# Group normalization on one core: transfers in runs of three, a part of the sums from TensorE to VectorE, and GpSimd's share of the scaling to VectorE

## The chip, the cores and the metric

The kernel runs on one core of a Trainium2 chip, alone. The metric is the device time of one execution in microseconds (us), the median of several executions. The time before the change was 633.9 us (633.54 to 634.19 in three runs).

## The reference

x has the shape (128, 1024, 32, 16) in bf16: 128 samples, 1024 channels in 32 groups. Each group of each sample (32 channels of 512 elements) is normalized with its own mean and variance, then each channel is scaled and shifted.

```python
G = 32
xr = x.reshape(B, G, C // G, H, W)
mu = xr.mean(axis=(2, 3, 4), keepdims=True)
var = ((xr - mu) ** 2).mean(axis=(2, 3, 4), keepdims=True)
xn = (xr - mu) / jnp.sqrt(var + 1e-5)
return xn.reshape(B, C, H, W) * g[None, :, None, None] + b[None, :, None, None]
```

The input and the output are 134 MB each, so the kernel must move 268.4 MB through the core's DMA engines. There is little arithmetic per byte.

## The kernel before

A tile has 128 partitions (4 samples x 32 groups) and 16384 columns (32 channels x 512), which is 4 MB. There are 32 tiles and six buffers. Per tile, TensorE sums the columns by multiplying 32 chunks of 512 columns with the identity into 512 columns of PSUM, VectorE reduces these to the mean, ScalarE squares the tile in two halves and sums the squares, and then 32 channels are scaled in place: 16 on VectorE, 13 on GpSimd, 3 on ScalarE. All loads and stores are issued from one queue (SP). The order of transfers is: six loads, then two stores, two loads, two stores, and so on ("runs of two").

```python
XBUFS = 6; UPFRONT = 6; RUN = 2; LAST_SHARE = 3; POOL_SHARE = 13
...
def matmuls(st, name, lo, hi):          # sums of chunks lo..hi-1 in PSUM
    ps = pspool.tile([P, MMN], F32, name=name)
    for k in range(lo, hi):
        nc.tensor.matmul(out=ps[:], lhsT=eye[:], rhs=st["xt"][:, k*MMN:(k+1)*MMN], ...)
...
def A(i):                               # scale the channels of tile i
    if not in_parts(i):                 # all but the last two tiles
        for n in range(POOL_SHARE):
            scale_on("pool", i, KC - LAST_SHARE - POOL_SHARE + n)
        for k in range(KC - LAST_SHARE - POOL_SHARE):
            scale_on("dve", i, k)
        ...
def finish(i):
    for k in range(KC - LAST_SHARE, KC):
        scale_on("act", i, k)           # one instruction per channel
    S(i, 0, NQ)                         # store tile i
    if i % RUN == RUN - 1:              # after each run of stores: a run of loads
        first = i + 1 + UPFRONT - RUN
        for j in range(first, min(first + RUN, NT)):
            L(j)
...
for i in range(NT):
    Q(i)                                # squares of tile i, finish(i - 1) in between
    if i + 1 < NT:
        M(i + 1); R0(i + 1)             # sums and mean of the next tile
    V(i)                                # variance, scale and shift of tile i
    A(i)
```

## Time and profile before

| | before |
|---|---|
| time, span in the profile | 633.9 us, 632.5 us |
| DMA | mean 425 GB/s over the span, 432 in the middle |
| ACT, DVE, POOL, PE busy | 85%, 60%, 55%, 41% |

In the views of the profile PE is TensorE and PEld its weight loads, DVE is VectorE, ACT is ScalarE, POOL is GpSimd, SP issues the transfers, and L368 is line 368 of the kernel. Here are three lines of the profile page of the kernel before: the busy time of each engine, and for 40 equal slices of the span the busy tenths of the DMA engines and what they moved.

```profile
PE 260.9 (41%) x1025; PEld 106.4 (17%) x1025; DVE 379.0 (60%) x645; ACT 537.9 (85%) x268; POOL 345.3 (55%) x523
...
DMA  9999999999999999999999999999999999999996
GB/s 371 437 428 406 436 433 431 433 429 433 429 424 433 429 437 431 432 434 433 434 432 424 432 433 431 429 432 432 431 431 431 436 429 432 431 425 435 431 423 260
```

DMA is at 9 (90% or more) in every slice but the last. The windows view says the same for the long middle part; its columns are each engine's busy time with its count of instructions, then TensorE's granted clock, the DMA share and GB/s.

```profile
core 0: us, PE busy (x) PEld busy (x) DVE busy (x) ACT busy (x) POOL busy (x), PEclk, DMA share, GB/s
113.00:543.00 430.00, 178.81 (x704) 72.86 (x704) 269.73 (x431) 379.11 (x185) 260.03 (x388) 0.71 1.00 432
```

So in this window the DMA share is 1.00, and every other engine has some time to spare (ACT, the busiest, is at 85% over the span). The next fence is from the DMA queues of the page (packets, bytes, share of the engines' time). Queue q1 carries the tiles; q8 and q14 carry instructions, in packets of 16 KB (q8) and 8 KB (q14), and the page counts their time with that of the same 16 DMA engines: 0.1% and 0.0%.

```profile
q1 hardware_dynamic: 10944, 268.44, 99.0%
q8 instruction: 8, 0.13, 0.1%
q14 instruction: 15, 0.12, 0.0%
```

The next fence has groups of instructions of the page, with busy time in all and the mean of one in ns.

```profile
L244 ACT ACTIVATE ja<-xt,negmean 128x8192 fp8e5<-128x8192 bf16 x60 | 426.6, 7109 | 55.2 <-DVE jd L189 55.1
...
L368 DVE TENSOR_SCALAR xt<-xt,scl,bia 128x512 bf16<-128x512 bf16 x536 | 351.4, 730 | 39.8 <-POOL bia L353 39.8
L368 POOL TENSOR_SCALAR xt<-xt,scl,bia 128x512 bf16<-128x512 bf16 x390 | 307.5, 801 | 3.4 <-POOL bia L353 0.3
...
L189 DVE TENSOR_SCALAR_CACHE_REDUCE jd<-pa 128x512 bf16<-128x512 f32 x32 | 21.9, 684 | 113.9 <-PE pa L166 113.9
```

One scaling instruction lasts 730 ns on VectorE and 801 ns on GpSimd here. On VectorE they overlap, so its pace is 0.66 us a channel (351.4 us over 536). The timeline of VectorE near the end shows the same 16 instructions once beside GpSimd (first line) and once alone (second line; the last two tiles use no GpSimd).

```profile
start us, us, engine line op out<-in xcount [idle before <-releaser]
574.64 11.11 DVE L368 TENSOR_SCALAR xt<-xt,scl,bia 128x512 bf16<-128x512 bf16 x16 [1.28 <-POOL bia L353]
...
591.62 5.26 DVE L368 TENSOR_SCALAR xt<-xt,scl,bia 128x512 bf16<-128x512 bf16 x16 [1.28 <-POOL bia L353]
```

They take 11.11 us beside GpSimd and 5.26 us alone: 0.69 against 0.33 us a channel. Why VectorE is slower beside GpSimd is not shown by the traces.

**Reading the landings.** In the trace each of the 76 loads and stores has 16 increments of its semaphore, and the page counts 16 DMA engines. I read each increment as the landing of one engine's share. That is my reading: the trace names no engine beside an increment. It fits the rate, as the first increments of loads that follow each other are 9.71 us apart, and 4.19 MB in 9.71 us is the 432 GB/s of the windows view. The times of the increments were read from the stored trace with a short script, as no view of the profile lists them. Sorted, they show how far the slowest DMA engine lags behind the fastest, though not which engine it is. For the last store of the kernel before, in us after the first of the 16 (which landed at 624.18):

```
0.00 0.05 0.21 0.82 1.56 1.62 1.71 1.71 1.84 2.97 3.13 3.22 4.13 5.26 7.03 7.36
```

In the first loads the lag is 0.5 us. The rest is built up in jolts (tiles for which the slowest engine takes 0.2 to 1.2 us longer than for the others), and the kernel ends with the slowest engine, at 631.54 us. The fastest engine takes 9.66 to 9.72 us for nearly every tile, with no gap.

### The profile page before, as it was taken

How to read it: one execution, taken by the hardware profiler on the slowest of the kernel's cores; microseconds unless marked ns; L12 is line 12 of the kernel's file. 1: busy time of each engine (PE TensorE's matmuls, PEld its weight loads, DVE VectorE, ACT ScalarE, POOL GpSimd, SP SyncE). 2: the span in 40 equal slices, each digit the busy share in tenths (PEclk: the TensorE clock that was granted, in tenths of full speed). 3: DMA queues.
4: the chain of work that ended last, by engine and by line, in shares of the span. 5: the costliest groups of instructions: out<-in, count | busy, mean ns of one | idle time of the engine just before them, and what ended most of it. 6: DMA issues, size and time to landing. Idle time of an engine off the chain costs nothing.

```text
span 632.5 us, 3907 instructions
## 1 busy us (share of the span) xinstructions
PE 260.9 (41%) x1025; PEld 106.4 (17%) x1025; DVE 379.0 (60%) x645; ACT 537.9 (85%) x268; POOL 345.3 (55%) x523
## 2 busy tenths in 40 slices
PE   5577609064180632806327063270723607146000
PEld 2223203021030210302113021030301203012000
DVE  1077766666676477563665636666466663657660
ACT  4599999999999699696996969969798796987960
POOL 0077776666666377563665636666365663657100
PEclk9789759668595675957759577595875958758555
DMA  9999999999999999999999999999999999999996
GB/s 371 437 428 406 436 433 431 433 429 433 429 424 433 429 437 431 432 434 433 434 432 424 432 433 431 429 432 432 431 431 431 436 429 432 431 425 435 431 423 260
DMA packets 11063, 268.70 MB, mean 425 GB/s; under 512 B 1312, under 2 KB 1312, under 8 KB 1312
## 3 DMA queue, kind: packets, MB, share of 16 engines
q1 hardware_dynamic: 10944, 268.44, 99.0%
q8 instruction: 8, 0.13, 0.1%
q14 instruction: 15, 0.12, 0.0%
q10 hardware_dynamic: 96, 0.00, 0.0%
HBM read 134.22 MB, written 134.22 MB: 424 GB/s over the span
## 4 chain that ended last, share of the span: by engine, by line
DMA 62%; ACT 15%; PE 9%; issue 5%; DVE 3%; POOL 2%; SPq 0%; DVEq 0%; ACTq 0%; POOLq 0%
DMA out_dram<-xt 40%; DMA xt<-in_x_dram 21%; ACT ja L244 13%; PE pa L166 9%; DVE xt L368 3%; ACT xt L363 2%; POOL xt L368 1%; DMA gb_b<-in_g_dram 0%; ACT rstd L308 0%; POOL scl L337 0%; POOL shift L343 0%; POOL bia L353 0%; SPq L101 0%; DVE rstd L312 0%; DVE jd L189 0%
## 5 line engine op out<-in xcount | busy, mean ns | idle before, releaser
L244 ACT ACTIVATE ja<-xt,negmean 128x8192 fp8e5<-128x8192 bf16 x60 | 426.6, 7109 | 55.2 <-DVE jd L189 55.1
L166 PE MATMUL pa<-xt,eye 128*128 128x512 bf16 x976 | 250.1, 421 | 317.9 <-DMA xt<-in_x_dram 317.9
L368 DVE TENSOR_SCALAR xt<-xt,scl,bia 128x512 bf16<-128x512 bf16 x536 | 351.4, 730 | 39.8 <-POOL bia L353 39.8
L368 POOL TENSOR_SCALAR xt<-xt,scl,bia 128x512 bf16<-128x512 bf16 x390 | 307.5, 801 | 3.4 <-POOL bia L353 0.3
L166 PEld LDWEIGHTS <-eye 128*128 128x128 bf16 x1024 | 106.3, 106 | 472.2 <-DMA xt<-in_x_dram 318.8
L337 POOL TENSOR_SCALAR scl<-gb,rstd 128x32 f32<-128x32 f32 x31 | 11.1, 358 | 220.1 <-DVE rstd L312 220.1
L189 DVE TENSOR_SCALAR_CACHE_REDUCE jd<-pa 128x512 bf16<-128x512 f32 x32 | 21.9, 684 | 113.9 <-PE pa L166 113.9
L363 ACT ACTIVATE xt<-xt,bia,scl 128x512 bf16<-128x512 bf16 x98 | 72.0, 799 | 0.8 <-DVE bia L324 0.8
L312 DVE RECIPROCAL rstd<-rstd 128x1 f32<-128x1 f32 x32 | 5.2, 163 | 72.7 <-ACT rstd L308 72.7
L244 ACT ACTIVATE ja<-xt,q 128x4096 fp8e5<-128x4096 bf16 x8 | 29.7, 3706 | 6.6 <-DVE jd L189 6.4
L343 POOL TENSOR_SCALAR shift<-scl,negmean 128x32 f32<-128x32 f32 x31 | 11.1, 358 | 3.1
L216 POOL TENSOR_SCALAR off<-negmean,q 128x1 f32<-128x1 f32 x2 | 0.9, 430 | 20.4 <-DVE jd L189 20.4
L166 PE MATMUL pb<-xt,eye 128*128 128x512 bf16 x48 | 11.0, 379 | 0.6 <-DMA xt<-in_x_dram 0.6
L244 ACT ACTIVATION_READ_ACCUMULATOR ja<-xt,negmean 128x1 f32 x60 | 11.2, 187 | 0.0
L308 ACT ACTIVATE rstd<-s,v 128x1 f32<-128x1 f32 x30 | 8.8, 294 | 2.8
L353 POOL TENSOR_TENSOR bia<-shift,gb 128x32 f32<-128x32 f32 x31 | 7.8, 251 | 2.6
L273 POOL TENSOR_SCALAR v<-s 128x1 f32<-128x1 f32 x30 | 5.7, 191 | 2.5
L308 ACT ACTIVATE rstd<-var,eps_t 128x1 f32<-128x1 f32 x2 | 0.6, 294 | 7.5 <-DVE jv L292 7.5
L156 DVE COPY gb<-gb_p 128x64 f32<-128x64 f32 x1 | 0.2, 225 | 5.5 <-PE gb_p L148 5.5
L116 ACT ACT_TABLE_LOAD x1 | 1.3, 1283 | 1.7 <-PEq L445 1.7
L189 DVE DVE_READ_ACCUMULATOR jd<-pa 128x1 f32 x32 | 2.6, 80 | 0.0
L292 DVE TENSOR_SCALAR_CACHE_REDUCE jv<-sq,seed 128x4 f32<-128x4 f32 x2 | 0.4, 214 | 2.7 <-ACT ja L244 2.7
(18 smaller groups left out, 6.1 us busy)
## 6 DMA issues: line engine op xcount, KB each, us to landing
xt<-in_x_dram SPq DMA_DIRECT2D x30, 4096.0 KB, 19.4
out_dram<-xt SPq DMA_DIRECT2D x30, 4096.0 KB, 29.3
xt<-in_x_dram SPq DMA_DIRECT2D x8, 1024.0 KB, 11.5
out_dram<-xt SPq DMA_DIRECT2D x8, 1024.0 KB, 17.9
gb_b<-in_g_dram ACTq DMA_DIRECT2D x1, 2.0 KB, 3.2
gb_b<-in_b_dram ACTq DMA_DIRECT2D x1, 2.0 KB, 5.2
```

The source lines that it names most:

```text
L116: chain("act", nc.scalar.activation(out=warm[:], in_=eps_t[:], func=ACT.Sqrt))
L166: nc.tensor.matmul(out=ps[:], lhsT=eye[:], rhs=st["xt"][:, k * MMN : (k + 1) * MMN], start=(k == lo), stop=(k == hi - 1),),
L189: nc.vector.tensor_scalar(out=jd[:], in0=ps[:], scalar1=-inv_n, scalar2=seed, op0=ALU.mult, op1=ALU.add, accum_out=total[:],),
L244: nc.scalar.activation(out=ja[:, 0:w], in_=st["xt"][:, k * w : (k + 1) * w], func=ACT.Square, bias=bias, scale=scale, accum_out=sq, satura ...
L273: nc.gpsimd.tensor_scalar(out=v0[:], in0=s0[:], scalar1=inv_n, scalar2=EPS, op0=ALU.mult, op1=ALU.add,),
L308: nc.scalar.activation(out=rstd[:], in_=last_sum[:], func=ACT.Sqrt, bias=bias[:], scale=scale),
L312: chain("dve", nc.vector.reciprocal(out=rstd[:], in_=rstd[:]))
L337: nc.gpsimd.tensor_scalar(out=scl[:], in0=gam, scalar1=rstd[:], scalar2=None, op0=ALU.mult),
L343: nc.gpsimd.tensor_scalar(out=shift[:], in0=scl[:], scalar1=st["negmean"][:], scalar2=None, op0=ALU.mult,),
L353: nc.gpsimd.tensor_tensor(out=bia[:], in0=shift[:], in1=bet, op=ALU.add),
L363: inst = nc.scalar.activation(out=span, in_=span, func=ACT.Identity, bias=bia, scale=scl)
L368: inst = eng.tensor_scalar(out=span, in0=span, scalar1=scl, scalar2=bia, op0=ALU.mult, op1=ALU.add,)
```

## The change

The intent is a kernel in which the transfers change direction less often and VectorE no longer scales beside GpSimd (0.69 against 0.33 us a channel above). The transfers go in runs of three (the first of two). TensorE sums only 12 chunks of most tiles; VectorE sums the other 20 in two passes, each of which adds two stretches of 2560 columns and accumulates. GpSimd scales nothing, and VectorE scales 29 channels. With the longer runs, the tile whose load and sum come in quarters is the first of the last run instead of the last tile. The diff, with cuts marked:

```diff
-RUN = 2
+RUN = 3
+FIRST_RUN = 2
-POOL_SHARE = 13
+PE_CHUNKS = 12
...
+    def shifted(i):
+        return i == 0 or i == NT - RUN
...
-            matmuls(st, "pa", 0, NMM)
+            matmuls(st, "pa", 0, NMM if pe_only(i) else PE_CHUNKS)
+    def pe_only(i):
+        return i == 0 or i >= NT - RUN
...
         else:
-            st["negmean"] = sum_of(st["pa"], None, "negmean")
+            w = (NMM - PE_CHUNKS) * MMN // 4
+            ...
+            for n in range(2):
+                first = PE_CHUNKS * MMN + n * 2 * w
+                nc.vector.scalar_tensor_tensor(
+                    out=jp[:], in0=st["xt"][:, first : first + w], scalar=1.0,
+                    in1=st["xt"][:, first + w : first + 2 * w],
+                    op0=ALU.mult, op1=ALU.add, accum_out=pairs[:, n : n + 1], ...)
+            part = sum_of(st["pa"], None, "part")
+            ...   # one small instruction adds part and the pairs: negmean
...
-            for n in range(POOL_SHARE):
-                scale_on("pool", i, KC - LAST_SHARE - POOL_SHARE + n)
-            for k in range(KC - LAST_SHARE - POOL_SHARE):
+            for k in range(KC - LAST_SHARE):
                 scale_on("dve", i, k)
...
-        if i % RUN == RUN - 1:
-            first = i + 1 + UPFRONT - RUN
-            for j in range(first, min(first + RUN, NT)):
+        if i % RUN == FIRST_RUN - 1:
+            done = i + 1 + UPFRONT
+            for j in range(max(UPFRONT, done - RUN), min(done, NT)):
                 L(j)
```

More of the change, by code (lines that the diff above doesn't have):

```diff
@@ L92 @@
     state = {}
+    def shifted(i):
+        return i == 0 or i == NT - RUN
     def L(i):
         xt = xpool.tile([P, F], BF16, name="xt")
-        parts = NQ if i == 0 or i >= NT - 1 else 1
+        parts = NQ if shifted(i) else 1
         w = F // parts
@@ L156, in GB @@
         chain("dve", nc.vector.tensor_copy(out=gb[:], in_=gb_p[:]))
-    def shifted(i):
-        return i == 0 or i == NT - 1
     def matmuls(st, name, lo, hi):
@@ L204, in R0 @@
             st["q"] = sum_of(st["pa"], None, "q")
-        else:
-            st["negmean"] = sum_of(st["pa"], None, "negmean")
+        elif pe_only(i):
+            st["negmean"] = sum_of(st["pa"], None, "negmean")
+        else:
+            w = (NMM - PE_CHUNKS) * MMN // 4
+            pairs = spool.tile([P, 2], F32, name="pairs")
+            jp = jpool.tile([P, w], FP8, name="jp")
+            for n in range(2):
+                first = PE_CHUNKS * MMN + n * 2 * w
+                chain(
+                    "dve",
+                    nc.vector.scalar_tensor_tensor(
+                        out=jp[:],
+                        in0=st["xt"][:, first : first + w],
+                        scalar=1.0,
+                        in1=st["xt"][:, first + w : first + 2 * w],
+                        op0=ALU.mult,
+                        op1=ALU.add,
+                        accum_out=pairs[:, n : n + 1],
+                        saturate=False,
+                    ),
+                )
+            part = sum_of(st["pa"], None, "part")
+            negmean = spool.tile([P, 1], F32, name="negmean")
+            jn = jpool.tile([P, 2], F32, name="jn")
+            chain(
+                "dve",
+                nc.vector.tensor_scalar(
+                    out=jn[:],
+                    in0=pairs[:],
+                    scalar1=-inv_n,
+                    scalar2=part[:],
+                    op0=ALU.mult,
+                    op1=ALU.add,
+                    accum_out=negmean[:],
+                ),
+            )
+            st["negmean"] = negmean
     def R1(i):
```

## The prediction

> **What bounds the kernel.** The DMA engines. The page's slices show DMA at 9 in 39 of 40, mean 425 GB/s[...]. Between 113 and 543 us the windows view gives DMA share 1.00 and 432 GB/s. ACT is busy 85%, DVE 60%, POOL 55%, PE 41%. One 4 MB tile takes 9.7 us per direction, 19.4 in and out; ACT needs about 16.9 (two squares of 7.1, three channels 2.1, small ones).

> I also took the sixteen landings of each DMA apart. The first engine's landings step by 9.71 (load) and 9.66 us (store), with no gap: 624.2 at the last store. The slowest engine drifts behind: 0.5 us in the first loads, 2.5 by 62 us, 5.7 by 410, 7.4 at the end (631.5), which is the span's end. The drift comes in jolts of 0.2 to 1.2 us, most in the last load of a pair, where loads give way to stores, or beside instruction-fetch packets (8 of 16 KB, 1.05 us each, on q8; 15 of 8 KB, 0.31 us, on q14). So the change can save only part of 7.4 us, 1.2%.

> **What the change does.**
> 1. Runs of three: load batches after the first six fall from 13 to 9. Jolts at the loads' end sum to about 2.9 us after the start; a third fewer saves about 1.
> 2. PE: 560 fewer matmuls. [...] 2050 PE instructions and 8 packets agree. About 930 remain: 4 packets fewer, about 4 us spread over 16 engines, 0.3 to 0.7 us on the slowest.
> 3. POOL's 13 channels (307 us in all) go. DVE's channels take 0.69 us beside POOL (16 in 11.1); alone, in the last tiles, 0.33 (16 in 5.26). 29 channels: 9.5 us.
> 4. Two paired passes over 2560 columns: estimate 2.9 us each, from the 512-column accumulate at 0.69 and the 4-column one at 0.21. DVE chain per tile: 9.5 + 5.9 + 0.8 + 0.3 + 0.2, plus the 1.3 wait for POOL's scale and shift: 18.0 us, under 19.4. DVE busy 80-85%, POOL about 6%.

> **Critical path.** Tile 4's store, needed at about 118 us, should be ready by about 113 (estimate); later the slack grows. In the tail the last tile's first store is needed about 614 and should issue near 608, as now (608.9). Nothing starves; the gain is 1 to 2 us of drift.

> **Prediction:** 632.3 us, 8 in 10 between 629.5 and 635.5. Faster by over 2%: 0.01; within 2%: 0.95; slower by over 2%: 0.04.

> **What would show it.** Right: DMA at 9 in every slice but the last; 432 GB/s or slightly more in the middle; last landing spread 5 to 7 us; 4 packets on q8; DVE scale step near 0.33 us; paired pass near 2.9 us. Wrong in step 4: passes over 3.6 us, waits of the DMA queue for DVE or ACT that leave DMA slices at 8 or lower.

> **What would make it wrong.** A paired pass at half speed (5.5 us) makes the DVE chain 23 us a tile: 15-20% slower. A late store in the first run of three costs a few us once. Or the drift is random from program to program and ends larger than 7.4 us.

633.9 us less about 1 us (step 1) and less 0.3 to 0.7 us (step 2) is 632.2 to 632.6 us, and it says 632.3. Step 2 can be read from the trace of the kernel before alone: 2050 TensorE instructions (1025 matmuls and 1025 weight loads) beside 8 packets on q8 are 256 for each packet, so 930 would need about four. The 2.9 us in step 4 is somewhat over what a straight line through the two measured instructions that it names gives (2.6 us), and the half speed among the risks is a supposition, not something a trace showed.

## The result, and the profile after

The changed kernel takes 635.98 us (635.83 to 637.06, four runs) beside 634.05 us for the kernel before: 1.0038 times as long, with a 95% interval from 1.0024 to 1.0052. Ratios here are the mean time of one kernel's fast runs over that of the other's in the same rounds, so they are not quite the ratio of the quoted medians. By the 2% rule this is as predicted, but it is 2 us on the wrong side: the prediction was a gain of 1 to 2 us, and the measured time is 0.5 us above its range.

The same lines of the page of the changed kernel:

```profile
PE 168.1 (27%) x456; PEld 57.9 (9%) x465; DVE 490.4 (77%) x1203; ACT 539.7 (85%) x268; POOL 45.0 (7%) x133
...
DMA  9999999999999999999999999999999999999994
GB/s 368 436 437 411 429 430 429 434 438 430 434 433 434 430 430 432 432 431 435 434 435 428 438 432 424 430 432 433 424 432 437 431 436 419 440 434 432 430 416 194
```

```profile
core 0: us, PE busy (x) PEld busy (x) DVE busy (x) ACT busy (x) POOL busy (x), PEclk, DMA share, GB/s
113.00:543.00 430.00, 100.94 (x247) 33.05 (x252) 359.81 (x858) 377.22 (x180) 31.93 (x91) 0.58 1.00 431
```

DMA is again at 9 everywhere but in the last slice, at 431 GB/s in the middle. No engine became the limit: VectorE is at 77%, ScalarE at 85%. The last slice moved 194 GB/s where it was 260 before. The queues and the groups:

```profile
q1 hardware_dynamic: 10944, 268.44, 98.6%
q14 instruction: 15, 0.12, 0.0%
q8 instruction: 3, 0.05, 0.0%
```

```profile
L283 ACT ACTIVATE ja<-xt,negmean 128x8192 fp8e5<-128x8192 bf16 x60 | 426.8, 7114 | 52.9 <-DVE jn L235 52.9
L407 DVE TENSOR_SCALAR xt<-xt,scl,bia 128x512 bf16<-128x512 bf16 x926 | 302.2, 406 | 39.8 <-POOL bia L392 39.8
...
L219 DVE SCALAR_TENSOR_TENSOR jp<-xt 128x2560 fp8e5<-128x2560 bf16 x56 | 157.9, 2820 | 46.8 <-DMA xt<-in_x_dram 45.9
...
L193 DVE TENSOR_SCALAR_CACHE_REDUCE jd<-pa 128x512 bf16<-128x512 f32 x32 | 22.0, 686 | 20.1 <-PE pa L167 20.1
...
L235 DVE TENSOR_SCALAR_CACHE_REDUCE jn<-pairs,part 128x2 f32<-128x2 f32 x28 | 6.0, 215 | 1.0
```

A channel takes VectorE 0.33 us (302.2 us over 926), a paired pass 2.82 us. Those steps came as predicted. TensorE's instructions on q8 fell from 8 packets to 3 (that q8 carries TensorE's is shown by e8 below: ten packets with 2560 TensorE instructions, none in e6 without them). q14 has 15 packets as before, but not the same ones: as the next paragraphs show, ten of them are VectorE's now and six were, so the other engines have five instead of nine. What VectorE waits for also shows that it is not too late:

```profile
engine line waited for: us in total, times, longest us
DVE jp L219 <- DMA xt<-in_x_dram: 45.9, 7, 7.0
DVE xt L407 <- POOL bia L392: 39.8, 31, 1.3
```

Its longest total wait is for loads, so VectorE is ahead of the DMA. The waits of the queue that issues the transfers did move to VectorE's scaling:

```profile
engine line waited for: us in total, times, longest us
SPq L420 <- DVE xt L407: 321.6, 29, 30.2
```

Before, it was 124.0 us in 14 waits. They cost nothing here, as other transfers were queued: the fastest DMA engine ended at 624.03 us, and at 624.18 before.

The landings of the last store tell where the 2 us are. The first of the 16 landed at 624.03 us, against 624.18 before; the lags are:

```
0.00 0.01 0.02 0.04 0.14 0.26 0.47 0.55 0.77 1.59 2.69 2.75 2.87 4.68 5.05 9.08
```

Compared rank by rank, fifteen DMA engines end earlier than before: the mean lag fell from 2.66 to 1.94 us. One engine ends at 633.11 us, 1.57 us later than the slowest before, and the spans differ by 1.6 us. From 231 us on this one engine is more than 1 us behind all the others, so it can be followed through the trace. Below is, for each packet on q14 or q8 in that part, how the lag of this slowest engine grew in the landing interval that the packet fell into, and how many VectorE instructions (semaphore instructions counted) had started by then:

```
packet at us   queue   VectorE instructions   lag grew by us
288.6          q14      574                   1.02  (a q8 packet in the same interval)
323.4          q14      634                   0.00
348.7          q14      695                   0.81
410.0          q14      819                   0.79
431.7          q14      865                   0.05
482.4          q14      963                   0.81
499.8          q8       985                  -0.01
540.4, 542.4   q14     1078, 1084             0.81
611.2          q14     1227                   0.79
```

The packets at 574, 695, 819, 963, 1084 (or 1078) and 1227 form a series, each about 115 to 145 VectorE instructions after the one before it in the series. Each of these has a jolt of 0.8 us or more, and the others have none. Going back to the start the series is 50, 187, 305, 457, 574 VectorE instructions (40.2, 104.5, 157.3, 229.7, 288.6 us), each with a jolt of 0.4 to 1.0 us; in that early part the slowest engine is not yet clear of the others, and it also has jolts beside no packet of the series (0.6 us at 63 us). Over the whole series a packet of 8 KB comes per 117 to 152 VectorE instructions. In e7 below, 2560 VectorE memsets came with 20 packets more on q14 than e6 without them, which is 128 instructions a packet; the spacing agrees. These are VectorE's own instruction fetches, and they all seem to fall on one and the same DMA engine. The changed kernel has 1241 VectorE instructions instead of 718, so ten such fetches instead of six.

### The profile page after: what moved, and what is told of

Its sections match the earlier page's. It is cut to its first block, busy times and chain, and to the rows that moved or that the text cites. A ratio compares the mean times of both kernels' runs of the same rounds, so it can differ in the third digit from the quotient of the medians.

```text
span 634.1 us, 2821 instructions
## 1 busy us (share of the span) xinstructions
PE 168.1 (27%) x456; PEld 57.9 (9%) x465; DVE 490.4 (77%) x1203; ACT 539.7 (85%) x268; POOL 45.0 (7%) x133
## 4 chain that ended last, share of the span: by engine, by line
DMA 56%; DVE 31%; ACT 5%; POOL 2%; PE 1%; issue 1%; SPq 0%; DVEq 0%; ACTq 0%
DMA out_dram<-xt 35%; DMA xt<-in_x_dram 21%; DVE xt L407 19%; DVE jp L219 10%; ACT ja L283 5%; PE pa L167 1%; DVE jd L193 1%; POOL scl L376 1%; POOL shift L382 1%; POOL bia L392 0%; SPq L105 0%; ACT xt L402 0%; DVE jn L235 0%; DVE rstd L351 0%; ACT rstd L347 0%
## 5 line engine op out<-in xcount | busy, mean ns | idle before, releaser
L407 DVE TENSOR_SCALAR xt<-xt,scl,bia 128x512 bf16<-128x512 bf16 x926 | 302.2, 406 | 39.8 <-POOL bia L392 39.8
L167 PE MATMUL pa<-xt,eye 128*128 128x512 bf16 x408 | 157.1, 561 | 412.8 <-DMA xt<-in_x_dram 404.2
L219 DVE SCALAR_TENSOR_TENSOR jp<-xt 128x2560 fp8e5<-128x2560 bf16 x56 | 157.9, 2820 | 46.8 <-DMA xt<-in_x_dram 45.9
L167 PEld LDWEIGHTS <-eye 128*128 128x128 bf16 x464 | 57.8, 130 | 522.5 <-DMA xt<-in_x_dram 415.5
L312 POOL TENSOR_SCALAR v<-s 128x1 f32<-128x1 f32 x30 | 12.9, 429 | 179.7 <-ACT ja L283 179.7
L235 DVE TENSOR_SCALAR_CACHE_REDUCE jn<-pairs,part 128x2 f32<-128x2 f32 x28 | 6.0, 215 | 1.0
L219 DVE DVE_READ_ACCUMULATOR jp<-xt 128x1 f32 x56 | 4.5, 80 | 0.0
```

The lines of the kernel that those rows point to most:

```text
L167: nc.tensor.matmul(out=ps[:], lhsT=eye[:], rhs=st["xt"][:, k * MMN : (k + 1) * MMN], start=(k == lo), stop=(k == hi - 1),),
L219: nc.vector.scalar_tensor_tensor(out=jp[:], in0=st["xt"][:, first : first + w], scalar=1.0, in1=st["xt"][:, first + w : first + 2 * w], op ...
L235: nc.vector.tensor_scalar(out=jn[:], in0=pairs[:], scalar1=-inv_n, scalar2=part[:], op0=ALU.mult, op1=ALU.add, accum_out=negmean[:],),
L312: nc.gpsimd.tensor_scalar(out=v0[:], in0=s0[:], scalar1=inv_n, scalar2=EPS, op0=ALU.mult, op1=ALU.add,),
L407: inst = eng.tensor_scalar(out=span, in0=span, scalar1=scl, scalar2=bia, op0=ALU.mult, op1=ALU.add,)
```

## The experiments

"Lag" below is the slowest DMA engine's last landing minus the fastest one's. Runs of one call shared a chip and the runs of the kernel before; those medians were 633.78, 633.87, 633.81 and 633.56 us in the four calls (e1 to e4, e5 to e8, e9 to e12, e13 to e15). By the 2% rule e7 is "unclear" and all others are "same"; what follows is about differences inside these 2%, and an interval that leaves out 1 shows that there is one. The results of e6 to e9 are wrong.

| run | what | time us | ratio to before (95% interval) |
|---|---|---|---|
| e1 | before, runs of three | 632.48 | 0.9978 (0.9964 to 0.9992) |
| e2 | changed, runs of two | 637.50 | 1.0056 (1.0043 to 1.0069) |
| e3 | before, VectorE scales 29 | 636.18 | 1.0036 (1.0023 to 1.0048) |
| e4 | before, 1200 tiny VectorE memsets | 642.93 | 1.0140 (1.0126 to 1.0153) |
| e5 | before, 1200 tiny GpSimd memsets | 635.81 | 1.0030 (1.0015 to 1.0045) |
| e6 | copy only | 631.47 | 0.9961 (0.9946 to 0.9976) |
| e7 | copy, 2560 VectorE memsets | 645.50 | 1.0208 (1.0151 to 1.0266) |
| e8 | copy, 2560 TensorE instructions | 632.64 | 0.9968 (0.9948 to 0.9988) |
| e9 | copy in runs of three | 629.15 | 0.9927 (0.9916 to 0.9939) |
| e10 | e1, a channel from VectorE to ScalarE | 632.37 | 0.9976 (0.9964 to 0.9988) |
| e11 | before, runs of four | 640.09 | 1.0098 (1.0080 to 1.0116) |
| e12 | changed, 6 channels back to GpSimd | 635.46 | 1.0024 (1.0011 to 1.0036) |
| e13 | e1, VectorE scales 29 | 635.15 | 1.0026 (1.0012 to 1.0040) |
| e14 | e13, 150 tiny VectorE memsets | 635.90 | 1.0037 (1.0025 to 1.0050) |
| e15 | changed, again | 635.93 | 1.0038 (1.0025 to 1.0051) |

### The parts of the change by themselves (e1, e2, e3)

e1 is the kernel before with only the order of transfers changed:

```diff
-RUN = 2
+RUN = 3
+FIRST_RUN = 2
-        if i % RUN == RUN - 1:
-            first = i + 1 + UPFRONT - RUN
-            for j in range(first, min(first + RUN, NT)):
+        if i % RUN == FIRST_RUN - 1:
+            done = i + 1 + UPFRONT
+            for j in range(max(UPFRONT, done - RUN), min(done, NT)):
```

> The kernel before with the runs of three alone (transfer order), no other change. Theory A (the loss is the drift of one DMA engine that carries VectorE's instruction fetches): VectorE's instructions are as before, so the time stays within 0.15% of before, 633 to 635 us, and the first engine still ends at 624. Rival B (longer runs cost time): 635.5 to 637, like the changed kernel.

It takes 632.48 us, 1.3 us less than before; the 0.5 us below the range given for Theory A come from the gain of the runs, which that text left out. Rival B is out: the runs of three save time. The fastest engine ended at 625.2 and not at 624 as expected: it waited for one of the last stores, by 0.6 us here and by 2 to 4 us in e5, e10, e13 and e14. The slowest engine was still busy then and lost nothing, so in these runs the lag at the end is smaller than the drift.

e2 is the changed kernel with only the order of transfers put back (the tail of the last three tiles is kept):

```diff
-RUN = 3
+RUN = 2
+TAIL = 3
-        return i == 0 or i == NT - RUN
+        return i == 0 or i == NT - TAIL
```

> The changed kernel with transfers in runs of two again. Theory A: VectorE still has over 1200 instructions and about ten fetches on one DMA engine, so the last landing is 8 to 10 us behind the first and the time stays at 635.5 to 637. Rival B (longer runs cost time): back to 633.5 to 634.5.

It takes 637.50 us, 1.5 us more than the changed kernel and 0.5 over Theory A's range. Its lag at the end was 7.1 us, not the 8 to 10 expected, because the fastest engine ended later too, at 627.2 (see e4). So the runs are worth 1.3 to 1.5 us in both kernels, roughly: e2 and the changed kernel ran in different calls, and their intervals overlap. And the rest of the change costs 3.7 us (637.50 less 633.78).

e3 moves GpSimd's channels alone:

```diff
-POOL_SHARE = 13
+POOL_SHARE = 0
```

> The kernel before with GpSimd's 13 channels moved to VectorE alone; sums and runs as before. VectorE gets about 1110 traced instructions in place of 718, so 9 fetches in place of 6. Theory A: slowest DMA engine about 2 us later, 635 to 637 us. Rival B (runs) and rival C (the paired passes' memory traffic slows DMA): no change, 633.5 to 634.5.

It takes 636.18 us: 2.4 us of the 3.7 come with the 389 more VectorE instructions, although VectorE needs less time for 29 channels alone (9.46 us in the changed kernel) than for 16 beside GpSimd (11.11 us). In its trace the slowest engine jolts by 0.75 to 1.0 us at 177, 244, 322, 400, 468, 542 and 612 us, each time with a q14 packet in the landing interval and 120 to 145 VectorE instructions after the one before.

### A dose of instructions (e4, e5)

e4 adds instructions that do nothing of use: one-column memsets after the scaling of each of 30 tiles. e5 is the same on GpSimd.

```diff
+            dose("dve", 40)     # 40 x nc.vector.memset(scratch[:], 0.0), [128, 1]
             if i + 1 < NT:
                 R1(i + 1)
```

> The kernel before plus 40 tiny VectorE memsets (one column) after each of 30 tiles: 1200 more VectorE instructions, about 9.4 more fetches, and nothing else; VectorE stays under the 19.4 us of a tile (2 to 3 us more per tile). Theory A: 9.4 x 0.8 = 7.5 us later on one DMA engine, 638 to 642 us, the other engines unchanged, the first engine's last landing still 624. Rivals B and C: unchanged, 633.5 to 634.5.

> The kernel before plus 40 tiny GpSimd memsets after each of 30 tiles: the control of the VectorE dose. If every 8 KB instruction fetch falls on one fixed DMA engine per issuing engine (theory A1): GpSimd's own DMA engine takes about 9 more fetches of 0.8 to 1.0 us, which makes it the slowest, 637 to 643 us. If only VectorE's fetches are bound to one engine (A2), or the dose of VectorE cost time through VectorE itself (rival D): 633.5 to 635.5.

e4 takes 642.93 us, 9.1 us more than before, somewhat over the range. The queues of its page show what was added, nine packets of 8 KB:

```profile
q8 instruction: 8, 0.13, 0.1%
q14 instruction: 24, 0.20, 0.1%
```

That is 1.0 us per fetch. From 123 us to the end, the slowest engine's steps from one tile to the next are 10.4 to 10.7 us in the intervals with a packet about every 120 VectorE instructions, and mostly 9.6 to 9.7 in the others. One expectation failed: the fastest engine ended at 632.8, not 624. With runs of two the lag stayed between about 7 and 8 us and then the others lost time too. The same is seen, smaller, in e2 and in e3 (fastest engine at 625.9, lag 7.5). In that order a load waits for the slowest engine's share of a store while only one more transfer is queued, so the others run out of work; this reason is argued from the order of issue and was not tested.

e5 takes 635.81 us, 1.9 us more, and falls between the two theories that its text named. Its q14 also had 24 packets instead of 15, and from 289 us on the slowest engine grew by 0.5 to 0.6 us in most intervals with a packet every 120 to 160 GpSimd instructions. So fetches of GpSimd also add up on the slowest engine, at a smaller cost each (0.5 to 0.6 us). Whether they all meet one engine, and why the cost is smaller, stays open.

### The transfers without the kernel (e6, e7, e8, e9)

e6 removes all computation. The stores write back what was loaded; loads, stores and their order are as before.

> Wrong result on purpose: the same loads and stores in the same order (runs of two), no computation at all; the output is a copy of x. The floor that the DMA engines set. Theory A: hardly any instruction fetches, so the last landing is only 1 to 3 us behind the first, 626.5 to 629.5 us. If the drift came from the switches between loads and stores alone: 632 to 634, as before.

This was a miss: 631.47 us, only 2.4 us less than before, where I expected 4 to 7. Its page has one instruction packet:

```profile
q1 hardware_dynamic: 10944, 268.44, 99.3%
q14 instruction: 1, 0.01, 0.0%
```

and still the last store has a lag of 5.4 us. So fetches are not the only cause of drift. In the copy, after the first run, every step of the slowest engine over 10 us (9.69 is normal) is in one place: the second load of a pair, which stores follow (10.02 to 10.66 us, landing at 179, 219, 258, 337, 415, 493 and 532 us). The change of direction from loads to stores is the second cause: it held the slowest engine up by 0.3 to 1.0 us at seven of 13 changes. e9 tests that by taking 9 such changes instead of 13 after the first, with the diff of e1 in the copy:

> Wrong result on purpose: the copy with transfers in runs of three. In the copy in runs of two, every jolt of the slowest DMA engine (0.3 to 1.0 us, 5 us in all) falls in the second load of a pair, the one that stores follow, and none beside a fetch. Theory S (each change from loads to stores costs the slowest engine about 0.4 us): 9 changes after the start in place of 13, so 1.0 to 2.0 us less than the copy's 631.5, 629.5 to 630.5. Rival (the jolts go with time or bytes, not with changes of direction): 631 to 632.

It takes 629.15 us, 2.3 us less than the copy in runs of two, slightly more than expected. It was run at another time. In its trace the slowest engine's steps over 10 us after the first run are again all in the last load of a run, three of them (10.17 to 10.55 us) where the copy in runs of two has seven. This is what the runs of three save. Why a load that stores follow is late on one engine was not tested.

e7 and e8 add instructions to the copy of e6 that nothing waits for: 2560 memsets on VectorE, or 1280 small matmuls with their 1280 weight loads.

```diff
+    for _ in range(2560):
+        nc.vector.memset(junk[:], 0.0)          # e7
...
+    for k in range(1280):
+        nc.tensor.matmul(out=ps[:], lhsT=eye[:], rhs=eye[:, 0:8], ...)   # e8
```

> The copy plus 2560 tiny VectorE memsets that nothing waits for: about 20 fetches of 8 KB. Theory A: 20 x 0.8 to 1.0 us on one DMA engine, 16 to 20 us more than the copy, 643 to 649 us. Rival D (VectorE's work itself is what costs time): no change from the copy, as nothing waits for VectorE.

> The copy plus 1280 tiny matmuls and 1280 weight loads (2560 PE instructions): about 10 fetches of 16 KB of about 1.0 us or a little more each. The traces of before and after put each of these on another DMA engine. Theory A: the slowest engine is 1 to 3 us later than in the copy alone, 627.5 to 632; if they too fell on one engine: 10 to 15 us more.

The first fence is a line of e7's queues, the second of e8's:

```profile
q14 instruction: 21, 0.17, 0.1%
```

```profile
q8 instruction: 10, 0.16, 0.1%
```

The 20 fetches of VectorE cost 14.0 us (645.50 less 631.47; four runs, one of them at 653.0), 0.7 us each. As nothing waits for VectorE in e7, Rival D is out. VectorE itself shows no cost: its memsets start every 125 ns without a gap at any of the 20 fetches. Its trace is the clearest evidence for Theory A. The first six fetches, from 10 to 90 us, took the slowest engine from 0.4 to 5.5 us behind the fastest, 0.86 us each, while the other fifteen stayed within 0.6 us: it is one engine. Up to the last fetch, at 314 us, each of the 19 whole tiles with a fetch in its interval took the slowest engine 10.45 to 11.11 us, and each of the 11 without one 9.48 to 9.72 us; after it no step is over 9.93 us. Later the other engines lost time as well, as in e4 (the fastest ended at 636.6, in e6 at 623.7). The ten fetches of TensorE, each twice the size, cost 1.2 us in all, and the runs of e8 spread by 2.4 us, so even that is not certain. In its trace they fell on about eight DMA engines: after the tenth, eight lag by 1.7 to 3.6 us and the other eight by 0.64 us or less. In the trace of the kernel before, the number of engines within 0.75 us of the fastest fell by one at each of its eight q8 packets, so these met eight different engines, as far as the landings can tell. In the trace of the changed kernel each of the three q8 packets pushes back a DMA engine that was not the slowest, by about 0.9 to 1.5 us.

### What is left over (e12, e13, e14, e15)

e12 gives 6 channels of the changed kernel back to GpSimd (180 fewer VectorE instructions):

```diff
+POOL_SHARE = 6
+            for n in range(POOL_SHARE):
+                scale_on("pool", i, KC - LAST_SHARE - POOL_SHARE + n)
-            for k in range(KC - LAST_SHARE):
+            for k in range(KC - LAST_SHARE - POOL_SHARE):
```

> The changed kernel with 6 of the 29 channels given back to GpSimd: 180 fewer VectorE instructions of 1241, so one or two fetches fewer on its DMA engine; GpSimd gets them on its own. Theory A: 0.8 to 1.8 us less than the changed kernel (635.98), 634.2 to 635.3. Rivals B (runs) and C (the memory traffic of the paired passes): no change, 635.8 to 636.5.

It takes 635.46 us, 0.5 us less than the changed kernel and less of a gain than expected. They were run at other times. So this agrees with Theory A in sign and settles little by itself.

The last question was whether the paired passes and the missing matmuls do anything beyond their instructions. e13 is e1 with POOL_SHARE = 0; e14 adds 5 tiny memsets per tile to it (the edit of e4, with 5 for 40; 30 waits that stood alone go into them), so that VectorE has 1227 instructions, 120 more, and fetches as often as the changed kernel; e15 is the changed kernel beside them.

> The kernel before with runs of three and with GpSimd's 13 channels on VectorE; TensorE still sums all 32 chunks, no paired passes. If the two effects add (runs of three -1.3, VectorE's 29 channels +2.4): 634.9, say 634.3 to 635.4.

> The same plus 5 tiny VectorE memsets after each of 30 tiles (150 instructions), so VectorE has about as many instructions as in the changed kernel, but TensorE still sums all chunks and there are no paired passes. Theory A (the instruction count of VectorE is all): one fetch more, 0.8 to 1.0 us over its neighbour without them and within 0.7 us of the changed kernel run beside it. If the paired passes or the fewer matmuls matter by themselves: further from the changed kernel than that.

> The changed kernel itself, beside the two above on the same chip: 635.6 to 636.6.

The times are 635.15, 635.90 and 635.93 us. The 150 memsets cost 0.75 us, and with them a kernel that has no paired pass and all of TensorE's matmuls takes the time of the changed kernel to within 0.03 us. The five runs of each spread by 0.8 to 1.0 us, so the agreement is good to about 0.5 us and no better. Within that, no cost of the passes' memory traffic is left to explain (Rival C), and no gain from five fewer TensorE fetches is seen; a small cost of the one and a small gain from the other could still cancel.

### Better versions (e10, e11)

e10 is e1 with LAST_SHARE = 4: ScalarE scales one channel more and VectorE one fewer, to save VectorE's last fetch.

> The kernel before with runs of three, and one channel more on ScalarE (4), one fewer on VectorE (15): 30 fewer VectorE instructions, so its sixth fetch, which came at its instruction 704 of 718, should not be needed. Theory A: 0 to 0.8 us less than runs of three alone (632.5), so 631.7 to 632.5; ScalarE's tile goes from 16.9 to 17.6 us, still under 19.4. If ScalarE is then too late: over 633.

It takes 632.37 us, 0.1 us less than e1: inconclusive between the two, but both beat the kernel before and the changed one. It was run at another time. Its q14 had 14 packets instead of 15.

e11 is e1 with RUN = 4.

> The kernel before with runs of four, the first of two. Theory S: 7 changes of direction in place of 9, 0.5 to 0.9 us less than runs of three, 631.6 to 632.0. Against it: the store of tile 5 is needed at 130 us, about when the tile is ready, and each later run leaves less time between a tile's load and its store; if compute is too late, 633 to 640 and DMA slices at 8 or lower.

It takes 640.09 us, and compute is too late. The waits of the DMA queue show it, first for e11 and then for the kernel before (columns: total us, times, longest):

```profile
engine line waited for: us in total, times, longest us
SPq L382 <- DVE xt L369: 505.9, 37, 36.9
SPq L102 <- DMA out_dram<-xt: 83.1, 14, 12.2
```

```profile
engine line waited for: us in total, times, longest us
SPq L101 <- DMA out_dram<-xt: 453.2, 26, 29.0
SPq L381 <- DVE xt L368: 124.0, 14, 37.0
```

In e11 the queue waits 505.9 us for VectorE's scaling, in 37 of its stores, and only 83.1 us for stores to land; before, it waited 453.2 us for stores to land. In the changed kernel 321.6 us of such waits left the fastest engine at 624.0 us, as transfers were queued, but here the queue ran dry: the fourth store of a run landed 10.1 to 11.6 us after the third even on the fastest engine, where 9.66 is normal, and the lag at the end is 0.15 us since all engines waited for the same thing. The slices of its GB/s dip at each such place, though the DMA digits stay at 9, contrary to what I expected:

```profile
GB/s 378 441 428 394 436 437 431 433 400 431 443 404 428 419 435 429 414 429 378 445 435 399 433 419 431 428 419 431 419 429 432 413 435 421 430 415 444 428 420 317
```

## Why the prediction was wrong

- **What bounds the kernel** was right: DMA at 9 throughout, the fastest engine ending at 624 before and after, all of the difference in the slowest engine.
- **Step 1, the runs of three**, was right in mechanism and size: about 1 us predicted, 1.3 to 1.5 measured (e1, e2), 2.3 in the bare copy (e6, e9).
- **Steps 3 and 4, VectorE's time**, were right: 0.33 us a channel, 2.82 us a pass (predicted 2.9), no starved transfer.
- **Step 2, the fetches, failed.** I counted TensorE's four (in fact five) fetches that go away, "about 4 us spread over 16 engines, 0.3 to 0.7 us on the slowest", and did not count the fetches of the 520 instructions that VectorE gains. (Four more at the jolt of 0.8 us are 3.2 us on that engine, an estimate.) I took every fetch to fall on any of the 16 engines alike. The runs showed the opposite for the two: TensorE's fetches spread over the DMA engines and cost the end almost nothing (ten of them 1.2 us, e8; five fewer no visible gain, e14 against e15), while VectorE's all delay one engine and add up (20 of them 14 us, e7; nine 9.1 us, e4).
- **The sum.** Runs -1.3 us, the 29 channels +2.4 us (e3), the instructions of the paired passes about +0.8 us (e14 less e13) make +1.9; the changed kernel was 1.9 us slower, and 2.4 in e15. e13, with the first two together, was +1.6 and not +1.1, so the sum holds to about 0.5 us. The prediction had -1 and -0.3 to -0.7 in it. Its last sentence named a drift that ends larger as a risk, but as a random one, which VectorE's part of it is not: in e15 the slowest engine jolted at the same instruction counts again, to within four.
- **What would show it.** The spread of 5 to 7 us was 9.1; q8 had 3 packets, not 4; VectorE was 77% busy, not 80 to 85.

Why VectorE's fetches all meet one DMA engine, and why a packet of 0.31 us holds its transfers up by 0.8 us or more, stays open. The record of the kernel before held the hint. It showed six fetches of VectorE, and in the last landings at 524 and 612 us a jolt of 0.75 to 0.86 us beside two of them.

## What to carry to other kernels

This kernel is bound by DMA (share 1.00 from 113 to 543 us), and its end was set by the slowest of the DMA engines, at 631.54 us before and 633.11 us after, while the fastest ended at 624. So read all 16 landings of a transfer and not only the mean rate: the two kernels moved 432 and 431 GB/s in the middle and ended 2 us apart. Count instructions as DMA traffic: moving many small instructions to one engine was not free here even where that engine had time to spare (VectorE is at 77% in the changed kernel; 389 more instructions on it cost 2.4 us in e3, 2560 cost 14.0 us in e7), because its fetches all held up the same DMA engine, as far as the landings can tell. Fewer changes between loads and stores saved a little (1.3 us in e1, 2.3 us in e9), as long as compute could keep the longer run of stores supplied; in e11 it could not, and the kernel lost 6.3 us.
